# Four PSUM banks for the second layer's first products, and a planner that knows which engine reads a bank

## The chip, the cores and the metric

The program runs on one core of a Trainium2 chip. A core has TensorE (PE, matrix products into the PSUM banks), VectorE (DVE), ScalarE (ACT), GpSimd (POOL) and SyncE (SP, which issues the transfers). The metric is the device time of one execution in microseconds (us). The kernel before took 1287.76 us (median of three runs, 1286.5 to 1288.33).

## The reference, cut to what matters

```python
scores = (q @ k.T) / sqrt(64)              # 4 batches, 8 heads, 768 positions, head size 64
keep   = (key < 4) | ((0 <= query - key) & (query - key < 128))
a      = softmax(where(keep, scores, -1e9))
x      = a @ v                             # as 3072 tokens x 512
h      = maximum(x @ w_in, 0);  y = (h * h) @ w_out         # first layer, 512 -> 2048 -> 512
h      = y @ w2_in;  g = h - tanh(h);  out = g @ w2_out     # second layer, the same sizes
```

Everything is float32. To keep that precision, an operand of a fast product is split into a high and a low part, and one product is made of three matmuls: high x high, high x low, low x high.

## The kernel before

**Tiling.** The first layer runs over 8 blocks of 384 tokens, the second over 6 blocks of 512. In both, the 2048 hidden columns are 16 chunks of 128. For a chunk, `mm_a` (line 567) makes the *first products*: 4 slices of 3 matmuls that add up in one PSUM bank. ACT and DVE turn that bank into g, split in two (`gh` and `gl`, in the second layer `g2h` and `g2l`). Then `mm_b` (line 581) makes the *second products*: 3 matmuls into each of the four banks `acc0` to `acc3`, which add up over all 16 chunks. So a chunk costs TensorE 24 matmuls, of 384 columns in the first layer and of 512 in the second.

**The banks.** There are eight: four `acc`, and `ph`, `S`, `T` and `O`. Attention uses `S` for scores, `T` for transposed weights and `O` for its output; the first layer's first products use `ph`. The second layer's first products use `ph` for even chunks and `S` for odd ones (line 569).

**The second layer's elementwise work** (`step2`, line 627): ACT reads the bank twice (u at L632, th at L633) and makes w from u (L635). DVE makes the mask mk (L639), r from bank and th (L637), w (L641), w times the bank (L643, the last reader of the bank), puts w into r where the mask says so (L645), then g2h (L260) and g2l (L268). The tiles u, th, w and mk have one buffer; r, g2h and g2l have two.

**Attention, as far as it matters here** (`scores` and `values`, lines 311 and 399): TensorE transposes one head's weights into `T` (L358, L359). The readers of `T` are a copy xe (L260 on DVE or L258 on ACT), its remainder (DVE, L370) and three small copies pts. POOL masks xe into pt (L374), and TensorE multiplies pt by the values into `O` (L410 to L415). Instructions of two engines that read the same bank wait for each other, in the order in which the kernel emits them.

**Weights.** A weight arrives as 64-bit words and is turned into two float32 parts by `w_split` (line 534): one instruction on ACT or DVE that reads the transferred words first (L549 or L551), three on DVE (L558, L560, L562), a copy (L258 or L260) and a remainder (L268). The second layer's weights are loaded and split during the last block of the first layer, into the places of the first layer's weights.

**What sets the order.** No order is written by hand. Each operation is put into `Order` with a priority and a cost for each engine that could do it. `solve` (line 124) walks through an imagined time and gives each engine the ready operation with the lowest priority number that it can start soon; where two engines could do an operation, it picks the one that would end sooner. The operations are then emitted in that order, and each engine works through its own list strictly in that order. A change of any cost or priority can therefore move instructions anywhere, and also from one engine to another.

Of the kernel before, what the change touches and what calls it, by code (L numbers as in the profile page):

```python
# [23 lines left out]
B, H, S, D = 4, 8, 768, 64  # L24
P = 128
NT, DM, DFF = B * S, H * D, 2048
NM = DFF // P
NE = DM // P
N1, N2 = 384, 512
NB1, NB2 = NT // N1, NT // N2  # L30
# [8 lines left out]
PLAIN = 2 * H  # L39


REBIAS = 2.0 ** -112


# [16 lines left out]


class Op:
    __slots__ = ("engs", "prio", "emit", "left", "deps", "out", "rank", "ready", "start", "eng", "end")


class C(tuple):
# [10 lines left out]
class Order:  # L78
# [9 lines left out]
    AHEAD = {"V": 1100.0, "D": 400.0}  # L88
    TICK, FIRST = 3413.0, 4590.0
    NEAR = 60.0  # L90
    SAFE = {"T": 250.0}

    def __init__(self):
# [2 lines left out]
    def add(self, engs, prio, reads, writes, emit):  # L96
        op = Op()
        op.engs, op.prio, op.emit, op.deps, op.out, op.rank = engs, prio, emit, set(), [], len(self.ops)
        for k in reads:
            if k in self.writer:  # L100
                op.deps.add(self.writer[k])
            self.readers.setdefault(k, []).append(op)
        for k in writes:
            if k in self.writer:
                op.deps.add(self.writer[k])
            op.deps.update(self.readers.pop(k, ()))
            self.writer[k] = op
        op.deps.discard(op)
        op.deps = sorted(op.deps, key=lambda d: d.rank)
        for d in op.deps:  # L110
            d.out.append(op)
        self.ops.append(op)
# [11 lines left out]
    def solve(self):  # L124
        free = {e: self.AHEAD.get(e, 0.0) for op in self.ops for e in op.engs}
        avail, pend = {e: [] for e in free}, {e: [] for e in free}
        tick = {int(self.FIRST // self.TICK): self.TICK}
        port = 0.0

        def offer(op):  # L130
            for e in op.engs:
                heapq.heappush(pend[e], (op.ready.get(e, 0.0), op.rank, op))

        for op in self.ops:
            op.left, op.ready, op.eng = len(op.deps), {}, None
        for op in self.ops:
            if not op.left:
                offer(op)

        def queue(g, item):  # L140
            return sum(i[2].engs[g][0] / len(i[2].engs) for i in avail[g] if i < item and i[2].eng is None)

        def begin(op, e, now):
            return max(now, port - 60.0) if op.engs[e][2] else now

        done, n = [], len(self.ops)
        while len(done) < n:
            e = min(free, key=lambda g: free[g])
            now, safe = free[e], self.SAFE.get(e, 0.0)
            while pend[e] and pend[e][0][0] <= now:  # L150
                _, r, op = heapq.heappop(pend[e])
                if op.eng is None:
                    heapq.heappush(avail[e], (op.prio, r, op))
            best, held, close, skipped = None, None, None, []
            while avail[e]:
                item = heapq.heappop(avail[e])
                op = item[2]
                if op.eng is not None:
                    continue
                at = begin(op, e, now)  # L160
                if all(max(free[g], op.ready.get(g, 0.0), port if op.engs[g][2] else 0.0) + queue(g, item) + op.engs[g][1] >= at + op.engs[e][1]
                       for g in op.engs if g != e):
                    if at <= now + self.NEAR:
                        if held is None or now + op.engs[e][0] <= held[0] + self.NEAR:
                            if op.ready.get(e, 0.0) + safe <= now:
                                best = item
                                break
                            close = close or item
                    elif held is None and close is None:
                        held = (at, item)  # L170
                skipped.append(item)
            if best is None:
                best = close or (held and held[1])
                if best:
                    skipped.remove(best)
            for item in skipped:
                heapq.heappush(avail[e], item)
            if best is None:
                later = [t for g, t in free.items() if g != e and t > now]
                if pend[e]:  # L180
                    later.append(pend[e][0][0])
                free[e] = min(later) if later else now + 1000.0
                continue
            best = best[2]
            at = begin(best, e, now)
            occ, took = self.clocked(tick, best.engs[e], at) if e == "T" else best.engs[e][:2]
            best.eng, best.start, best.end = e, at, at + took
            free[e] = at + occ
            if best.engs[e][2]:
                port = max(port, at + occ)  # L190
            done.append(best)
            for d in best.out:
                for g in d.engs:
                    d.ready[g] = max(d.ready.get(g, 0.0), best.end + self.hop(e, g))
                d.left -= 1
                if not d.left:
                    offer(d)
        self.order = sorted(done, key=lambda o: o.start)
        return max(op.end for op in done)
# [34 lines left out]
def c_mm(*ns, slow=1):  # L234

    t = sum(slow * (n * 0.4355 + 6.0) for n in ns)
    return C(t, t + 165.0)


class Fast:  # L240
# [144 lines left out]
    def least(self, prio, reads, writes, src, out, nm, half, i, scale):  # L385

        nc = self.nc
        m = self.c["m"][0 if half == 0 and i == 0 else 1 if half == 0 and i == 1 else 2]
        self.o.add({"V": C(222, 375)}, prio, reads, writes,
                   lambda e: nc.vector.tensor_tensor_reduce(out=out(), in0=src(), in1=m, op0=ALU.add, op1=ALU.min, scale=scale,  # L390
                                                            scalar=3.0e38, accum_out=nm()))

# [141 lines left out]
    def w_split(self, layer, m, part, prio, k):  # L534
# [9 lines left out]
        def words(i):  # L544
            return self.wraw[at].rearrange("p (n t) -> p n t", t=2)[:, :, i]

        def rebias(e):
            if e == "A":
                nc.scalar.activation(out=tf, in_=words(1).bitcast(F32), func=AF.Copy, scale=REBIAS)  # L549
            else:  # L550
                nc.vector.tensor_scalar(out=tf, in0=words(1).bitcast(F32), scalar1=REBIAS, scalar2=None, op0=ALU.mult)  # L551

# [13 lines left out]

    def mm_a(self, layer, t, n, prio):
        nc, N = self.nc, (N1, N2)[layer]
        pb = ("ph", 0) if layer == 0 or n % 2 == 0 else ("S", 0)
        x = "x2" if layer else "x"  # L570
        for c in range(NE):
            def emit(e, c=c):
                ph = self.bank[pb]
                w, xh, xl = self.wt[n, 0], self.t[x + "h", t % 2], self.t[x + "l", t % 2]
                for k, (a, b) in enumerate(((0, xh), (0, xl), (512, xh))):
                    nc.tensor.matmul(out=ph[:, :N], lhsT=w[:, a + c * P:a + (c + 1) * P], rhs=b[:, c, :],  # L576
                                     start=(c == 0 and k == 0), stop=(c == NE - 1 and k == 2))
            self.o.add({"T": c_mm(N, N, N)}, prio + 0.1 * c, [("w", n, 0, 0), ("w", n, 0, 1), (x + "h", t % 2, c), (x + "l", t % 2, c)], [pb], emit)
        return pb
# [46 lines left out]

    def step2(self, t, n, v):
        nc, o, T = self.nc, self.o, self.t
        pb = self.mm_a(1, t, n, v)
        k = n % 2  # L630
        th, u, w, mk, r, gh, gl = ("th", 0), ("u", 0), ("w", 0), ("mk", 0), ("r2", k), ("g2h", k), ("g2l", k)
        o.add({"A": c_act(N2, True)}, v + 1.5, [pb], [u], lambda e: nc.scalar.activation(out=T[u], in_=self.bank[pb], func=AF.Square))  # L632
# [238 lines left out]
def general_in(tc, pool, raw, w, out, cst, bank, fl):  # L871
# [25 lines left out]
    for layer in range(2):  # L897
        for m in range(NM):
            for part in range(2):
# [4 lines left out]
                lo, hi, tf = words[:, :, 0], words[:, :, 1], t.bitcast(F32)  # L904
                v.tensor_scalar(out=tf, in0=hi.bitcast(F32), scalar1=REBIAS, scalar2=None, op0=ALU.mult)
                v.tensor_scalar(out=t, in0=t, scalar1=3, scalar2=0x7FFFFFF8, op0=ALU.logical_shift_left, op1=ALU.bitwise_and)
# [157 lines left out]
```

## Time and profile before

| | |
|---|---|
| median of the runs | 1287.76 us (1286.5 to 1288.33) |
| the profiled execution | 1288.81 us, of which the span from first to last instruction is 1286.8 us |
| PE busy | 1255.7 us, 98% of the span |
| DVE, ACT, POOL busy | 1031.0, 630.8 and 152.3 us |
| mean granted clock of TensorE | 0.996 of full speed |

The page of the profile says at the top that TensorE is busy nearly all the time: 1286.8 - 1255.7 = 31.1 us of the span are without a matmul. The share alone doesn't say what those 31.1 us wait for, so the rows further down are taken from the stretches in which they lie. Three views are used. Busy time by stretch gives, for each engine, microseconds and (x) instructions, then the granted clock of TensorE, the share of the transfer engines and GB/s. The timeline gives start, duration, engine, line, operation and tiles; a bracket at its end is the time for which the engine sat idle just before, and the instruction that ended it. The list of waits sums such idle time by pair of lines: microseconds, times, longest.

### The profile page before, as it was taken

How to read it: one execution, taken by the hardware profiler on the slowest of the kernel's cores; microseconds unless marked ns; L12 is line 12 of the kernel's file. 1: busy time of each engine (PE TensorE's matmuls, PEld its weight loads, DVE VectorE, ACT ScalarE, POOL GpSimd, SP SyncE). 2: the span in 40 equal slices, each digit the busy share in tenths (PEclk: the TensorE clock that was granted, in tenths of full speed). 3: DMA queues.
4: the chain of work that ended last, by engine and by line, in shares of the span. 5: the costliest groups of instructions: out<-in, count | busy, mean ns of one | idle time of the engine just before them, and what ended most of it. 6: DMA issues, size and time to landing. Idle time of an engine off the chain costs nothing.

```text
span 1286.8 us, 18762 instructions
## 1 busy us (share of the span) xinstructions
PE 1255.7 (98%) x6568; PEld 1114.6 (87%) x6568; DVE 1031.0 (80%) x2488; ACT 630.8 (49%) x1493; POOL 152.3 (12%) x195
## 2 busy tenths in 40 slices
PE   8899999999999999999999999999999999999997
PEld 5688999999999999999999978888888888888886
DVE  6899997877777777777769999977877877877775
ACT  5655765655555556555535565533433423432332
POOL 1211222222112221122211100000000000000000
PEclk9999999999999999999999999999999999999999
DMA  6884122211222212122118820100100200000000
GB/s 208 276 297 160 32 67 73 84 56 51 75 60 65 76 51 77 52 59 84 28 54 288 286 85 1 36 31 1 66 1 1 66 1 1 34 1 1 33 1 35
DMA packets 41718, 95.01 MB, mean 74 GB/s; under 512 B 4752, under 2 KB 18576, under 8 KB 41616
## 3 DMA queue, kind: packets, MB, share of 16 engines
q1 hardware_dynamic: 41472, 93.34, 22.9%
q8 instruction: 53, 0.87, 0.3%
q10 hardware_dynamic: 144, 0.40, 0.1%
q14 instruction: 49, 0.40, 0.1%
HBM read 79.56 MB, written 14.16 MB: 73 GB/s over the span
## 4 chain that ended last, share of the span: by engine, by line
PE 77%; DVE 10%; issue 5%; DMA 3%; POOL 2%; ACT 2%; DVEq 0%; SPq 0%; ACTq 0%; POOLq 0%
PE ph L576 23%; PE acc L592 21%; PE acc L590 12%; PE S L576 10%; POOL pt L374 2%; PE O L413 2%; PE O L520 2%; DMA yd<-y 1%; DVE wd L560 1%; PE T L358 1%; PE S L324 1%; DMA wr<-w 1%; PE S L325 1%; PE wide L458 1%; PE S L458 1%
## 5 line engine op out<-in xcount | busy, mean ns | idle before, releaser
L576 PE MATMUL ph<-xh,w 128*128 128x384 f32 x1024 | 339.7, 345 | 6.5 <-DVE r L608 3.2
L590 PE MATMUL acc<-gh,w 128*128 128x384 f32 x1024 | 322.4, 339 | 1.5 <-ACT y L258 1.4
L592 PE MATMUL acc<-w,g2h 128*128 128x512 f32 x768 | 299.1, 393 | 1.0 <-DVE g2h L260 1.0
L576 PEld LDWEIGHTS ph<-xh,w 128*128 128x128 f32 x1024 | 192.3, 189 | 10.3 <-DVE r L608 4.7
L590 PEld LDWEIGHTS acc<-gh,w 128*128 128x128 f32 x1024 | 190.5, 188 | 2.4 <-ACT y L258 2.2
L592 PEld LDWEIGHTS acc<-w,g2h 128*128 128x128 f32 x768 | 144.4, 188 | 34.3 <-DVE g2h L260 1.5
L590 PE MATMUL acc<-gl,w 128*128 128x384 f32 x512 | 172.8, 337 | 0.8 <-DVE gl L268 0.7
L576 PE MATMUL ph<-xl,w 128*128 128x384 f32 x512 | 172.3, 337 | 0.4 <-DVE xl L268 0.4
L592 PE MATMUL acc<-w,g2l 128*128 128x512 f32 x384 | 153.0, 398 | 0.7 <-DVE g2l L268 0.7
L576 PE MATMUL ph<-x2h,w 128*128 128x512 f32 x384 | 150.9, 395 | 2.4 <-DVE w L643 2.4
L576 PE MATMUL S<-x2h,w 128*128 128x512 f32 x384 | 151.1, 395 | 0.0
L374 POOL TENSOR_SCALAR_AFFINE_SELECT pt<-xe 128x768 fp32r<-128x768 f32 x96 | 82.6, 885 | 346.5 <-DVE xe L370 346.5
L632 ACT ACTIVATE u<-ph 128x512 f32<-128x512 f32 x48 | 28.7, 598 | 154.5 <-PE ph L576 153.9
L639 DVE TENSOR_SCALAR mk<-u 128x512 uint8<-128x512 f32 x96 | 40.8, 425 | 73.8 <-ACT u L632 73.8
L590 PEld LDWEIGHTS acc<-gl,w 128*128 128x128 f32 x512 | 96.3, 188 | 2.4 <-DVE gl L268 2.2
L576 PEld LDWEIGHTS ph<-xl,w 128*128 128x128 f32 x512 | 97.0, 189 | 1.1 <-DVE xl L268 0.6
L334 ACT ACTIVATE cb<-cb,nm 128x132 f32<-128x132 f32 x144 | 58.3, 405 | 67.0 <-DVE nm L390 65.1
L632 ACT ACTIVATE u<-S 128x512 f32<-128x512 f32 x48 | 28.7, 599 | 125.2 <-PE S L576 124.6
L576 PEld LDWEIGHTS ph<-x2h,w 128*128 128x128 f32 x384 | 72.1, 188 | 19.9 <-DVE w L643 2.7
L592 PEld LDWEIGHTS acc<-w,g2l 128*128 128x128 f32 x384 | 72.2, 188 | 19.4 <-DVE g2l L268 1.3
L576 PEld LDWEIGHTS S<-x2h,w 128*128 128x128 f32 x384 | 72.1, 188 | 17.2
L606 ACT ACTIVATE r<-ph 128x384 f32<-128x384 f32 x115 | 56.4, 491 | 57.0 <-PE ph L576 54.9
(176 smaller groups left out, 2380.6 us busy)
## 6 DMA issues: line engine op xcount, KB each, us to landing
wr<-w SPq DMA_DIRECT2D x64, 512.0 KB, 5.4
raw<-raw SPq DMA_DIRECT2D x32, 454.0 KB, 3.4
raw<-raw SPq DMA_DIRECT2D x31, 390.0 KB, 3.2
yd<-y SPq DMA_DIRECT2D x40, 192.0 KB, 2.0
raw<-yd SPq DMA_DIRECT2D x28, 256.0 KB, 3.2
out<-y SPq DMA_DIRECT2D x20, 256.0 KB, 2.0
raw<-raw SPq DMA_DIRECT2D x24, 160.0 KB, 2.3
raw<-raw SPq DMA_DIRECT2D x24, 128.0 KB, 2.1
```

Of the source, the lines that this page charges most:

```text
L324: nc.tensor.matmul(out=bank[sb][:, :n], lhsT=lhs, rhs=kh[:, col:col + n], start=True, stop=False)
L334: lambda e, i=i: nc.scalar.activation(out=t[cb][:, i, :], in_=t[cb][:, i, :], func=AF.Exp, bias=t[nm][:, i:i + 1], scale=-1.0, accum_out=t ...
L374: lambda e, u=u, s=s, sign=sign, op=op: nc.gpsimd.affine_select(out=t[pt].rearrange("p (n t) q -> p n t q", t=2)[:, 2 * u:, s, :], in_=t[x ...
L413: nc.tensor.matmul(out=oo[:, c:c + cnt * P], lhsT=vv[:, b - 2, :], rhs=pt[:, k + 2 * l:k + 2 * l + 3 * cnt - 2:3, :], start=(n == 0 and l ...
L458: lambda e, i=i, col=N1 + col, n=n: nc.tensor.matmul(out=place(i)[:, :n], lhsT=t["raw", q][:, i * P:(i + 1) * P], rhs=t["raw", q][:, col:c ...
L520: nc.tensor.matmul(out=out[:, c:c + cnt * P], lhsT=v[:, b, :], rhs=t[pp][:, sl:sl + cnt, :], start=(n == 0), stop=False)
L576: nc.tensor.matmul(out=ph[:, :N], lhsT=w[:, a + c * P:a + (c + 1) * P], rhs=b[:, c, :], start=(c == 0 and k == 0), stop=(c == NE - 1 and k ...
L590: nc.tensor.matmul(out=acc[:, :N1], lhsT=w[:, a + e_ * P:a + (e_ + 1) * P], rhs=g, start=st, stop=sp)
L592: nc.tensor.matmul(out=acc, lhsT=g[:, e_ * P:(e_ + 1) * P], rhs=w[:, a:a + 512], start=st, stop=sp)
L606: nc.scalar.activation(out=r, in_=ph, func=AF.Relu)
L632: o.add({"A": c_act(N2, True)}, v + 1.5, [pb], [u], lambda e: nc.scalar.activation(out=T[u], in_=self.bank[pb], func=AF.Square))
L639: lambda e: nc.vector.tensor_scalar(out=T[mk], in0=T[u], scalar1=U_MAX, scalar2=None, op0=ALU.is_lt))
```

## The change

Five edits, all in the planner's model or in what it is told:

1. `mm_a` takes the banks S, O, T and ph in turn for the second layer's chunks, where it took ph and S.
2. The first products of chunks 0 to 2 of the second layer's first block get a priority lower by 25 (earlier), and those of chunks 14 and 15 of its last block one lower by 8.
3. The planner keeps, for each PSUM bank, when and on which engine it was last used, and lets another engine's operation begin only after that (`lock`, `banks`, `begin`).
4. A matmul that follows an idle moment of TensorE is taken to cost 100 ns more (`AFRESH`).
5. The planned time until the result of `least` is there is 296 ns, where it was 375.

The arithmetic is the same, and so is the number of instructions of each kind of work.

```diff
+EARLY = 25.0, 8.0
...
+        op.banks = sorted({k for k in (*reads, *writes) if k[0] in ("acc", "ph", "S", "T", "O", "wide")}) if "T" not in engs else []
...
         def begin(op, e, now):
+            for k in op.banks:
+                end, g = lock.get(k, (0.0, e))
+                if g != e:
+                    now = max(now, end + self.hop(g, e))
             return max(now, port - 60.0) if op.engs[e][2] else now
...
-                if all(max(free[g], op.ready.get(g, 0.0), port if op.engs[g][2] else 0.0) + queue(g, item) + op.engs[g][1] >= at + op.engs[e][1]
+                if all(max(begin(op, g, free[g]), op.ready.get(g, 0.0)) + queue(g, item) + op.engs[g][1] >= at + op.engs[e][1]
...
+            if e == "T" and at > last:
+                occ, took = occ + self.AFRESH, took + self.AFRESH
...
+            for k in best.banks:
+                lock[k] = best.end, e
...
-        self.o.add({"V": C(222, 375)}, prio, reads, writes,
+        self.o.add({"V": C(222, 296)}, prio, reads, writes,
...
-        pb = ("ph", 0) if layer == 0 or n % 2 == 0 else ("S", 0)
+        pb = ("ph" if layer == 0 else ("S", "O", "T", "ph")[n % 4], 0)
...
-        pb = self.mm_a(1, t, n, v)
+        pb = self.mm_a(1, t, n, v - (EARLY[0] if t == 0 and n < 3 else EARLY[1] if t == NB2 - 1 and n >= NM - 2 else 0.0))
```

The order of the instructions differs from the first attention heads on. Three places follow, before and after. Line numbers are 13 higher after the change.

**DVE at the end of the first layer.** `gl` is the low part of the first layer's last chunk. `mk`, the first `r`, `w` and `g2h`, `g2l` belong to chunk 0 of the second layer, `wd` and `w_9`, `w_10`, `w_11` to weights being split, and `y` to the first layer's output. Before, from `gl` on:

```order
L268 TENSOR_TENSOR gl_172<-r_168,gh_170 128x384
L562 SCALAR_TENSOR_TENSOR wd_176<-wr_8_1_7124,wd_176 128x512
L558 TENSOR_SCALAR wd_175<-wd_175 128x512
L260 COPY y_173<-acc_458 128x384
L268 TENSOR_TENSOR w_8_1_7404<-wd_176,w_8_1_7404 128x512
L560 SCALAR_TENSOR_TENSOR wd_175<-wr_10_0_7151,wd_175 128x512
L260 COPY y_174<-acc_459 128x384
L562 SCALAR_TENSOR_TENSOR wd_175<-wr_10_0_7151,wd_175 128x512
L639 TENSOR_SCALAR mk_7369<-u_7367 128x512
L637 TENSOR_TENSOR r_7370<-ph_462,th_7366 128x512
```

and after, from `mk` on:

```order
L652 TENSOR_SCALAR mk_7430<-u_7428 128x512
L575 SCALAR_TENSOR_TENSOR wd_175<-wr_11_0_7246,wd_175 128x512
L650 TENSOR_TENSOR r_7431<-S_476,th_7427 128x512
L281 TENSOR_TENSOR gl_172<-r_168,gh_170 128x384
L654 SCALAR_TENSOR_TENSOR w_7429<-w_7429,u_7428 128x512
L650 TENSOR_TENSOR r_7432<-O_62,th_7427 128x512
L656 TENSOR_TENSOR w_7429<-w_7429,S_476 128x512
L281 TENSOR_TENSOR w_11_0_7467<-wd_175,w_11_0_7467 128x512
L658 COPY_PREDICATED r_7431<-mk_7430,w_7429 128x512
L571 TENSOR_SCALAR wd_176<-wd_176 128x512
L273 CAST g2h_7433<-r_7431 128x512
L652 TENSOR_SCALAR mk_7430<-u_7428 128x512
```

Chunk 0's work began eight rows behind `gl`; now it begins three rows ahead of it, and the weights are further on by then.

**PE at the end of the second layer's last block.** `w_15_0` stands for the first products of the last chunk, `w_12_1` to `w_14_1` for second products. Before, from the last group of first products on:

```order
L576 MATMUL S_463<-x2h_6662,w_15_0_7867 128x512
L576 MATMUL S_463<-x2l_6664,w_15_0_7867 128x512
L576 MATMUL S_463<-x2h_6662,w_15_0_7867 128x512
L592 MATMUL acc_461<-w_13_1_7819,g2h_7373 128x512
L592 MATMUL acc_461<-w_13_1_7819,g2l_7375 128x512
L592 MATMUL acc_461<-w_13_1_7819,g2h_7373 128x512
L592 MATMUL acc_458<-w_14_1_7895,g2h_7372 128x512
```

and after, from the same group on:

```order
L589 MATMUL ph_475<-x2h_6672,w_15_0_7887 128x512
L589 MATMUL ph_475<-x2l_6674,w_15_0_7887 128x512
L589 MATMUL ph_475<-x2h_6672,w_15_0_7887 128x512
L605 MATMUL acc_474<-w_12_1_7764,g2h_7433 128x512
L605 MATMUL acc_474<-w_12_1_7764,g2l_7435 128x512
L605 MATMUL acc_474<-w_12_1_7764,g2h_7433 128x512
L605 MATMUL acc_471<-w_13_1_7850,g2h_7434 128x512
```

The last first products are now made one chunk earlier: ahead of the second products of chunk 15 there stood 15 matmuls (one bank of chunk 13 and all of chunk 14), and now there stand 27.

**DVE at a head's transposed weights in `T`**, in the stretch where attention and first layer run side by side. Before:

```order
L260 CAST gh_170<-r_168 128x384
L260 CAST pts_1249<-T_61 8x128
L268 TENSOR_TENSOR gl_172<-r_168,gh_170 128x384
L370 TENSOR_TENSOR xe_1247<-T_61,xe_1247 128x3x128
L390 ISA cb_1238,nm_1240<-S_463,m_76 128x132
```

and after, at such a head:

```order
L403 ISA nm_1251 128x1
L383 TENSOR_TENSOR xe_1259<-T_61,xe_1259 128x3x128
L273 CAST pts_1262<-T_61 8x128 x2
L273 CAST gh_169<-r_167 128x384
L281 TENSOR_TENSOR gl_172<-r_168,gh_170 128x384
```

Before, every head's remainder of xe came behind all three copies pts. After, it comes ahead of two of them at 14 of the 48 heads. At the other heads it still comes last, mostly with all three copies pts on ACT.

## Rows read from the trace of the kernel before

**Rows 1.** Busy time by stretch, around the layer change, later, and the sum.

```profile
700.00:800.00 100.00, 95.72 (x467) 83.98 (x466) 96.56 (x179) 59.94 (x107) 9.90 (x7) 1.00 0.44 141
800.00:900.00 100.00, 100.00 (x433) 80.89 (x432) 83.88 (x144) 38.83 (x70) 0.00 (x0) 1.00 0.07 22
...
1260.00:1287.00 27.00, 19.67 (x83) 15.03 (x81) 14.02 (x24) 7.43 (x13) 0.00 (x0) 0.94 0.12 42
sum 1287.00, PE 1255.66 PEld 1114.56 DVE 1031.01 ACT 630.78 POOL 152.26; mean PE 59.79 PEld 53.07 DVE 49.10 ACT 30.04 POOL 7.25
```

**Rows 2.** Timeline, TensorE at the start of the second layer.

```profile
742.85 0.34 PE L590 MATMUL acc<-gl,w 128*128 128x384 f32 x1
...
748.74 0.50 PE L576 MATMUL ph<-x2h,w 128*128 128x512 f32 x1 [2.41 <-DVE w L643]
...
752.42 0.50 PE L592 MATMUL acc<-w,g2l 128*128 128x512 f32 x1 [0.43 <-DVE g2l L268]
```

**Rows 3.** Timeline, VectorE at the start of the second layer.

```profile
741.83 0.55 DVE L268 TENSOR_TENSOR gl<-r,gh 128x384 fp32r<-128x384 f32 x1
...
746.14 0.42 DVE L639 TENSOR_SCALAR mk<-u 128x512 uint8<-128x512 f32 x1
746.48 0.68 DVE L637 TENSOR_TENSOR r<-ph,th 128x512 f32<-128x512 f32 x1
...
751.68 0.69 DVE L268 TENSOR_TENSOR g2l<-r,g2h 128x512 fp32r<-128x512 f32 x1
```

**Rows 4.** Chain of waits, start of the second layer (start, duration, engine, tiles).

```profile
743.99 3.89 DMA yd<-y
```

**Rows 5.** Timeline, the end of the second layer.

```profile
1272.87 0.60 ACT L632 ACTIVATE u<-S 128x512 f32<-128x512 f32 x1 [3.88 <-PE S L576]
...
1273.60 0.39 PE L592 MATMUL acc<-w,g2l 128*128 128x512 f32 x1
...
1277.35 0.50 PE L592 MATMUL acc<-w,g2h 128*128 128x512 f32 x1 [1.03 <-DVE g2h L260]
...
1278.08 0.50 PE L592 MATMUL acc<-w,g2l 128*128 128x512 f32 x1 [0.23 <-DVE g2l L268]
```

**Rows 6.** Timeline, one head's transposed weights and what follows.

```profile
316.30 0.30 PE L359 MATMUL T<-idr,ask 128*96 128x128 f32 x1
...
317.21 0.28 DVE L260 CAST pts<-T 8x128 fp32r<-8x128 f32 x1 [0.22 <-ACT xe L258]
...
317.52 0.53 ACT L258 CAST pts<-T 8x128 fp32r<-8x128 f32 x2 [0.35 <-DVE pts L260]
...
318.15 0.56 DVE L370 TENSOR_TENSOR xe<-T,xe 128x384 fp32r<-128x384 f32 x1 [0.66 <-ACT pts L258]
...
320.83 0.50 PE L413 MATMUL O<-pt,vv 128*128 128x256 f32 x2 [0.28 <-POOL pt L374]
```

**Rows 7.** List of waits, TensorE's and VectorE's for such heads.

```profile
PE O L413 <- POOL pt L374: 1.8, 8, 0.3
...
DVE xe L370 <- ACT pts L258: 15.2, 40, 0.7
```

**Rows 8.** Timeline, TensorE's long waits in the first 200 us.

```profile
47.43 0.71 PE L458 MATMUL S<-raw 128*128 128x260 f32 x2 [1.39 <-DVE pnm L390]
...
50.66 0.70 PE L458 MATMUL S<-raw 128*128 128x260 f32 x2 [1.56 <-DVE pnm L390]
...
117.29 0.44 PE L576 MATMUL ph<-xh,w 128*128 128x384 f32 x1 [1.42 <-DVE xh L260]
```

**Rows 9.** Busy time in two stretches of 4 us behind such waits.

```profile
52.00:56.00 4.00, 4.00 (x17) 2.89 (x17) 3.13 (x10) 2.29 (x6) 0.00 (x0) 0.62 0.59 233
120.00:124.00 4.00, 4.00 (x17) 4.00 (x16) 3.47 (x9) 1.57 (x5) 0.00 (x0) 0.59 0.46 122
```

**Rows 10.** Timeline of ScalarE, then the page's table of transfers: weights.

```profile
676.12 0.66 ACT L549 ACTIVATE wd<-wr 128x512 f32<-128x512 f32 x1 [3.40 <-DMA wr<-w]
...
wr<-w SPq DMA_DIRECT2D x64, 512.0 KB, 5.4
```

More of the change, by code (lines that the diff above doesn't have):

```diff
@@ L63 @@
 class Op:
-    __slots__ = ("engs", "prio", "emit", "left", "deps", "out", "rank", "ready", "start", "eng", "end")
+    __slots__ = ("engs", "prio", "emit", "left", "deps", "out", "rank", "banks", "ready", "start", "eng", "end")
 class C(tuple):
@@ L90 @@
     NEAR = 60.0
+    AFRESH = 100.0
     SAFE = {"T": 250.0}
@@ L127, in solve @@
         tick = {int(self.FIRST // self.TICK): self.TICK}
-        port = 0.0
+        port, lock, last = 0.0, {}, 0.0
         def offer(op):
@@ L186, in solve @@
             occ, took = self.clocked(tick, best.engs[e], at) if e == "T" else best.engs[e][:2]
+            if e == "T" and at > last:
+                occ, took = occ + self.AFRESH, took + self.AFRESH
             best.eng, best.start, best.end = e, at, at + took
             free[e] = at + occ
+            if e == "T":
+                last = free[e]
             if best.engs[e][2]:
                 port = max(port, at + occ)
+            for k in best.banks:
+                lock[k] = best.end, e
             done.append(best)
```

## The prediction

> **What bounds the kernel now.** I read busy time by stretch first. The sum row gives TensorE 1255.66 us of work in a span of 1286.8, so 31.1 us are without a matmul, and only there (or where the clock is low) can time be won [rows 1]. From 800 to 900 us, the second layer in its steady course, TensorE is busy for 100.00 of 100 us at a granted clock of 1.00, with 433 matmuls, 0.231 us each; the reader should see that nothing waits there, though two banks serve the first products. From 700 to 800 us, at the layer change, it is different: DVE is busy for 96.56 us and TensorE for 95.72, so DVE, which splits weights, ends the first layer and begins the second, sets the pace.
>
> The timelines then name the waits. At the start of the second layer, first products stand 2.41 us until DVE's last reader of `ph` (L643) is done, and second products 0.43 us for g2l: 2.84 us [rows 2]. At the end, chunk 15's second products wait 1.03 us for g2h and 0.23 us for g2l: 1.26 us [rows 5]. The list of waits has 8 waits of the value products for POOL's pt, 1.8 us together [rows 7]. Ahead of 200 us there are three long ones, 1.39, 1.56 and 1.42 us, all on DVE [rows 8], and behind them two stretches of 4 us at a granted clock of 0.62 and 0.59 [rows 9]: a mix of the two levels, 2.4 and 1.2 GHz, following TensorE's idle moments, which costs 4 x 0.38 = 1.5 and 4 x 0.41 = 1.6 us.
>
> **The change, part by part.**
>
> *Steady second layer: 0.* Four banks instead of two give each chunk's readers more time, but TensorE has no idle time to give back there [rows 1]. The Trainium skill ("Perfetto Trace Analysis", section "Optimizing Tensor Performance", "Matmuls") says that independent matmul groups should rotate through different PSUM banks, so that emptying one overlaps the next group; by that sentence the whole layer would gain, and the 100.00 busy us show that two banks already give that overlap here.
>
> *The end.* Chunk 15's bank is read from 1272.87 on, and its g2h releases TensorE at 1277.35: 4.48 us [rows 5]. Before, 15 matmuls stand between its last first product and its second products, 15 x 0.231 = 3.5 us; after, 27, so 12 x 0.231 = 2.8 us more cover against 1.26 us of wait. The first matmul behind each wait also lasts 0.50 instead of 0.39 us [rows 5], 0.2 us for two. Chunks 13, 14 and 15 now come closer together on DVE, whose tiles u, th, w and mk have one buffer; the first products of 13 and 14 finish 0.7 us apart, by the matmuls that stand between them in the order. Adding the durations of the DVE steps in that order leaves some 0.7 to 1 us of the cover over. I take -1.5. Bounds: -1.5, or +0.5 if chunk 15's elementwise work is pushed back by more than the cover.
>
> *The start of the second layer.* Lost now: 2.84 plus 0.2 for two first matmuls of 0.50 us, 3.0. After, chunks 0, 1 and 2 make their first products during the first layer's last chunks, in S, O and T, and chunk 3 in `ph`, so no bank has to be emptied before the second products of the last first-layer chunk. Is DVE on time for these, with three chunks' elementwise work now mixed in? In the order TensorE has 30 more matmuls ahead of them (30 x 0.231 = 6.9 us later) and DVE has 14 more instructions ahead of `gl`; at 96.56 / 179 = 0.54 us each [rows 1] 7.5, by their kinds 7.1. `gl` now ends at 742.38 [rows 3] and is used at 742.85 [rows 2], 0.47 us of lead; 0.1 to 0.6 us of shift use up some or all of that. Next come chunk 0's second products: g2l begins 9 rows behind `gl`, 9 x 0.54 = 4.9 us, where it now begins at 751.68, 9.85 us behind [rows 3]. TensorE has 12 matmuls of 384 columns (0.175 us apart, 2.1) and 9 of 512 (2.1) to do in between, 4.2 us. So it may wait up to 0.3 to 0.6 us there. The output copies y, which empty the four `acc` banks, stand in the way too: their transfer takes 3.89 us [rows 4], and y has two buffers, so the third and fourth copies, DVE's among them, may be late by 0 to 1 us. I leave 1.1 us lost: gain 1.9. Bounds: -3.1 (nothing lost), +0.5 (a copy y that waits on DVE's list and holds `gl`'s successors too).
>
> *Attention's `T` bank.* In the head shown, from the transposing matmul at 316.30 to the value products at 320.83 it takes 4.53 us, through a chain that hops between ACT and DVE since both read `T` [rows 6]; VectorE sits 15.2 us in 40 such waits [rows 7], which matters only where TensorE waits at the end, 1.8 us in 8. In the new order, where less TensorE work than about 4.5 us lies between, the remainder of xe precedes two of the copies pts (0.6 to 1 us off the chain); the others have more. I take -1.3 of the 1.8. Bounds: -1.8, +0.7 (half a wait per head at the same eight places, 0.1 us each: the largest now is 0.3).
>
> *The first 200 us.* At the places of the three waits of [rows 8] the order of TensorE's rows is the same and DVE's steps ahead of them alike, so 0; but attention's front is replanned, and a wait there shifts by its own size: 1.4 to 1.6 either way, with a clock dip of 1.5 that comes or goes: -3 to +3.
>
> *The rest: 0.* About 40 instructions move from DVE to ACT; ACT is busy for 630.78 us of the span [rows 1].
>
> Sum: -1.5 - 1.9 - 1.3 = -4.7. The profiled execution took 1288.81 us, the median of the runs is 1.05 lower: 1287.76 - 4.7 = 1283.1.
>
> **The rivals.**
>
> *R1, the same DVE work waits elsewhere: 1286.3.* DVE is busy for 96.56 of 100 us at the layer change [rows 1]. If what TensorE no longer waits for on a bank it waits for on gl and g2l, since DVE's list has no slack, the start gains nothing; the value products likewise wait for POOL behind another reader. Only the end's 1.5 is left. For it speaks the DVE share, against it that DVE still stands idle for 3.44 of these 100 us, which steps issued earlier can fill.
>
> *R2, slower, weights: 1291.* In the order DVE now does 6 of the first weight steps that touch transferred words, before 2 (the rest on ACT). A transfer takes 5.4 us to land, and ACT stood 3.40 us for one [rows 10]. When DVE stands, `gl`, r and g2l stand behind it in its list, and TensorE behind them. Two such waits are 6.8 us; this decides once they exceed the 4.7 of the forecast: 1283.1 + 6.8 + about 1 for a clock dip = 1291. Against it: DVE was idle for only 3.44 of these 100 us, so most words are there in time.
>
> *R3, more gained: 1280.1.* If the wait at 117 us (1.42) [rows 8] and the clock dip behind it (1.6) [rows 9] dissolve with the new order, 3.0 more goes. The same local order speaks against it.
>
> *R4, the clock: 1292.* If the rotation let TensorE's clock drop at the start of each of six second-layer blocks, 6 x 1.5 = 9 us [rows 9]. Against it: at 800 to 900 us the target bank already changes every 3 matmuls, first to second products and back, at a clock of 1.00 and with no idle time [rows 1]. The Trainium skill ("TensorE: Matmul & The Clock Gate", section "A second HAM failure mode: psum-queue depth-cycling") describes a kernel whose cycling through banks made TensorE idle in short moments and its clock oscillate; that would be this rival.
>
> **How the numbers follow.** Forecast 0.53, R3 0.10, R1 0.22, R2 0.11, R4 0.04. A difference of 0.2%, 2.6 us, is about what a measurement of this kernel can tell from none. Faster by more: the forecast and R3, 0.63. Within: R1, 0.22. Slower: R2 and R4, 0.15. The likeliest's own range is 1280.3 to 1285.2, from its bounds taken together; the range for 8 times in 10 goes from R3 with one more wait of 1.5 gone to between R1 and R2: 1278.6 to 1289.2.
>
> **What would show it.** The end: no gap on TensorE between the last first product and the end. The start: a gap of up to about 1 us, with g2l or a copy y named, in place of 2.41 for L643 (then L656). Attention: fewer than 8 waits for pt, under 0.5 us together. Steady second layer: still 100.00, the clock 1.00. If the sum is right and these are not, I was lucky; a new wait of over 2 us between 700 and 760 us, or DVE waiting for transferred weights there, makes the forecast wrong, and so would waits before 200 us of other sizes than [rows 8].

## The result, and the profile after

The changed kernel took 1266.95 us (median of four runs, 1265.11 to 1269.36), the kernel before beside it 1288.05: ratio 0.9839, 95% interval 0.982 to 0.9858. The forecast was 1283.1 with a range down to 1278.6, so the direction was right and the size wrong: 21.1 us came off where 4.7 were forecast. The profiled spans are 1286.8 and 1263.1 us, 23.7 apart.

Busy time by stretch of the changed kernel (us, TensorE busy and its matmuls, then weight loads, DVE, ACT, POOL, granted clock, share of the transfers, GB/s) answers [rows 1]:

```profile
700.00:800.00 100.00, 99.92 (x470) 85.16 (x470) 99.72 (x187) 59.61 (x106) 0.00 (x0) 1.00 0.30 95
800.00:900.00 100.00, 100.00 (x432) 80.87 (x432) 81.52 (x138) 37.52 (x67) 0.00 (x0) 1.00 0.11 32
...
1240.00:1263.10 23.10, 17.51 (x76) 13.81 (x74) 12.21 (x21) 7.67 (x13) 0.00 (x0) 0.94 0.14 49
sum 1263.10, PE 1244.08 PEld 1113.16 DVE 1023.16 ACT 644.24 POOL 143.22; mean PE 59.24 PEld 53.01 DVE 48.72 ACT 30.68 POOL 6.82
```

The sum row holds the surprise. The span lost 23.7 us, but TensorE's idle time only 31.1 - 19.0 = 12.1; the other 11.6 went out of its *busy* time, though the same 6568 matmuls are made at the same clock. So "busy" held waits. One view of one stretch tells where. From 200 to 700 us, where attention and the first layer run side by side, before:

```profile
200.00:700.00 500.00, 494.40 (x3007) 481.54 (x3007) 377.74 (x1149) 276.40 (x748) 100.50 (x124) 1.00 0.25 75
```

and after:

```profile
200.00:700.00 500.00, 498.75 (x3071) 494.06 (x3070) 388.71 (x1133) 296.21 (x804) 101.25 (x125) 1.00 0.28 83
```

TensorE's busy time rose by 4.4 us, but 64 more matmuls fitted in, and the weight loads' busy time rose by 12.5 us. How a wait hides is seen in one head of the kernel before (timeline, TensorE and its weight loads):

```profile
287.81 0.33 PE L590 MATMUL acc<-gl,w 128*128 128x384 f32 x1
...
287.99 0.34 PE L590 MATMUL acc<-gh,w 128*128 128x384 f32 x1
288.48 0.30 PEld L413 LDWEIGHTS O<-pt,vv 128*128 128x128 f32 x2 [0.47 <-POOL pt L374]
288.48 0.50 PE L413 MATMUL O<-pt,vv 128*128 128x256 f32 x2
288.70 0.19 PEld L410 LDWEIGHTS O<-pt,vv 128*128 128x128 f32 x1
288.82 0.28 PE L410 MATMUL O<-pt,vv 128*128 128x256 f32 x1
```

A matmul of 384 columns is shown as busy for 0.34 us, but the next one starts 0.17 to 0.18 us after it. Here the next one starts 0.49 us later, 0.32 late, and the matmul's own row shows no bracket, since the row before seems to cover most of it. The weight load's row does show it: 0.47 us for POOL's pt.

So I went from start to start instead: each matmul's distance to the next one, less that of an undisturbed matmul of its width (0.173 us for 384 columns, 0.230 for 512, 0.117 for 256, 0.118 for 260). The undisturbed course adds up to 1197 us in both kernels; what lies beyond it is 82.4 us before and 58.9 after, 23.5 less, nearly the whole difference of the spans. The levels hang on what is taken for the narrower matmuls (with other choices 200 to 700 us holds from 16.6 to 38.3 us before); the differences do not, that stretch loses 12.8 us with each of them. By stretch (us beyond the undisturbed course; "locks and banks" is an experiment further down):

| stretch | before | after | difference | forecast | locks and banks |
|---|---|---|---|---|---|
| 0 to 200, front | 47.5 | 43.3 | -4.2 | 0 | 40.4 |
| 200 to 700, attention with first layer | 22.2 | 9.4 | -12.8 | -1.3 | 9.2 |
| 700 to 760, layer change | 5.9 | 1.6 | -4.3 | -1.9 | 0.4 |
| 760 to 1240, second layer | 4.6 | 4.4 | -0.2 | 0 | 4.3 |
| 1240 to the end | 2.2 | 0.2 | -2.0 | -1.5 | 0.2 |

The profiled execution of before (1288.81 us) lies above its median and that of the changed kernel (1265.11) is the fastest of its four, so the differences of this table come out some us larger than those of the medians.

From 200 to 700 us, delays ahead of the value products (O) fell from 7.3 to 0.4 us, ahead of second products (acc) from 5.1 to 1.5, ahead of scores (S) from 3.5 to 1.2. The weight loads' list of waits (us in total, times, longest) says the first of these directly. Before:

```profile
PEld O L413 <- POOL pt L374: 8.7, 19, 0.6
```

and after:

```profile
PEld O L426 <- POOL pt L387: 0.6, 4, 0.2
```

The list of the matmuls' own waits had 1.8 us in 8 for the same thing [rows 7]. What became of a head, in the changed kernel's timeline, answers [rows 6]:

```profile
318.28 0.30 PE L372 MATMUL T<-idr,ask 128*96 128x128 f32 x1
318.67 0.48 ACT L271 CAST xe<-T 128x384 fp32r<-128x384 f32 x1 [0.17 <-PE T L372]
319.05 0.79 ACT L271 CAST pts<-T 8x128 fp32r<-8x128 f32 x3
319.93 0.56 DVE L383 TENSOR_TENSOR xe<-T,xe 128x384 fp32r<-128x384 f32 x1 [0.34 <-issue]
320.56 1.78 POOL L387 TENSOR_SCALAR_AFFINE_SELECT pt<-xe 128x768 fp32r<-128x768 f32 x2 [8.48 <-DVE xe L383]
...
322.90 0.39 PE L426 MATMUL O<-pt,vv 128*128 128x256 f32 x2
```

All three copies pts follow xe on ACT, in 0.79 us; before, the readers of T went ACT to DVE to ACT to DVE. From the first reader's start to the end of xe's remainder the median head took 2.02 us before and takes 1.76 after. DVE's longest wait of [rows 7], 15.2 us in 40, is halved:

```profile
DVE xe L383 <- ACT pts L271: 7.5, 26, 1.2
```

The value products start 4.62 us after the transposes, with 4.5 us of other matmuls between. Before, 18 of 48 heads had only 3.7 or 4.0 us of matmuls there and 21 had 4.3; after, 35 have 4.5 us or more (before 9), and the 11 with 3.7 or 4.0 all have the remainder of xe ahead of two copies pts.

The end has no wait left on TensorE: the timeline from 1238 us on shows no bracket on its rows, where [rows 5] had 1.26 us. By the lists of waits, DVE waits for no transferred weights, and ACT once, 3.0 us at 659 us, before the layer change.

### The profile page after: what moved, and what is told of

It reads as the page before. It is cut to its first block, busy times and chain, and to the rows that moved or that the text cites. A ratio compares the mean times of both kernels' runs of the same rounds, so it can differ in the third digit from the quotient of the medians.

```text
span 1263.1 us, 18806 instructions
## 1 busy us (share of the span) xinstructions
PE 1244.1 (98%) x6568; PEld 1113.2 (88%) x6568; DVE 1023.2 (81%) x2453; ACT 644.2 (51%) x1541; POOL 143.2 (11%) x192
## 4 chain that ended last, share of the span: by engine, by line
PE 88%; DVE 7%; issue 2%; ACT 1%; DMA 1%; POOL 0%; DVEq 0%; POOLq 0%; ACTq 0%
PE ph L589 23%; PE acc L605 21%; PE acc L603 18%; PE T L589 5%; PE S L589 5%; PE O L589 5%; PE O L426 2%; PE S L338 1%; PE S L337 1%; PE T L371 1%; PE O L533 1%; DVE wd L573 1%; DVE wd L575 1%; DVE w L281 1%; PE O L428 1%
## 5 line engine op out<-in xcount | busy, mean ns | idle before, releaser
L605 PE MATMUL acc<-w,g2h 128*128 128x512 f32 x768 | 295.8, 396 | 0.0
L619 ACT ACTIVATE r<-ph 128x384 f32<-128x384 f32 x120 | 59.1, 492 | 80.4 <-PE ph L589 78.8
L589 PE MATMUL T<-x2h,w 128*128 128x512 f32 x192 | 75.0, 390 | 0.0
L589 PE MATMUL O<-x2h,w 128*128 128x512 f32 x192 | 74.9, 391 | 0.0
L589 PE MATMUL S<-x2h,w 128*128 128x512 f32 x192 | 74.7, 391 | 0.0
L589 PE MATMUL ph<-x2h,w 128*128 128x512 f32 x192 | 74.6, 391 | 0.0
L658 DVE COPY_PREDICATED r<-mk,w 128x512 f32<-128x512 uint8 x96 | 71.9, 749 | 2.7
L281 DVE TENSOR_TENSOR gl<-r,gh 128x384 fp32r<-128x384 f32 x128 | 70.9, 554 | 2.5 <-ACT gh L271 1.5
```

What stands on the lines that cost most here:

```text
L281: (nc.vector if e == "V" else nc.gpsimd).tensor_tensor(out=out, in0=a, in1=b.bitcast(F32), op=ALU.subtract)
L605: nc.tensor.matmul(out=acc, lhsT=g[:, e_ * P:(e_ + 1) * P], rhs=w[:, a:a + 512], start=st, stop=sp)
L619: nc.scalar.activation(out=r, in_=ph, func=AF.Relu)
L658: lambda e: nc.vector.copy_predicated(out=T[r], mask=T[mk], data=T[w]))
```

## The experiments

Times are medians beside the kernel before on the same chip: 1285.64 us for the first four, 1286.37 for the next four, 1286.01 for the last three. "Beyond the undisturbed course" always stands against the profile of before shown above. Where a diff below has the changed kernel's lines taken back, it is against the changed kernel.

**Locks only.**

```diff
-    AFRESH = 100.0
+    AFRESH = 0.0
-EARLY = 25.0, 8.0
+EARLY = 0.0, 0.0
-        self.o.add({"V": C(222, 296)}, prio, reads, writes,
+        self.o.add({"V": C(222, 375)}, prio, reads, writes,
-        pb = ("ph" if layer == 0 else ("S", "O", "T", "ph")[n % 4], 0)
+        pb = ("ph", 0) if layer == 0 or n % 2 == 0 else ("S", 0)
```

> The kernel before with edit 3 alone: the planner knows that two engines can't read one PSUM bank at a time; the old banks, no priorities, no AFRESH, the old time for least. From start to start of TensorE's matmuls, 200 to 700 us holds 22.2 us beyond the even course before and 9.4 after the change. Theory L (the locks removed that): 200 to 700 us falls to about 9 to 11, the front by 2 to 4, start and end of the second layer stay as before: 1270 to 1275 us. Rival F (the matmul behind an idle moment priced higher did it): 1285 to 1289. Rival S (the gain needs all edits together, it is the luck of one order): anywhere over 1278.

Measured: 1270.29 us, 15.4 below, ratio 0.9881 (0.9862 to 0.99). Beyond the undisturbed course 200 to 700 us holds 10.9 us (before 22.2), the layer change 5.4 and the end 2.0 (before 5.9 and 2.2): theory L. The front gained 9.6, far more than the 2 to 4 expected; the profiled execution is the fastest of the four here too. The same stretch of its profile as above:

```profile
200.00:700.00 500.00, 497.41 (x3065) 494.39 (x3065) 377.11 (x1089) 313.55 (x856) 102.22 (x125) 1.00 0.27 85
```

3065 matmuls and 494.39 us of weight loads: edit 3 alone has the changed kernel's middle, and F and S fall. In its order 37 of 48 heads read T as ACT, ACT, ACT, ACT, DVE; before, one did.

**Banks and priorities only.**

```diff
-        op.banks = sorted({k for k in (*reads, *writes) if k[0] in ("acc", "ph", "S", "T", "O", "wide")}) if "T" not in engs else []
+        op.banks = sorted({k for k in (*reads, *writes) if k[0] in ()})
-    AFRESH = 100.0
+    AFRESH = 0.0
-        self.o.add({"V": C(222, 296)}, prio, reads, writes,
+        self.o.add({"V": C(222, 375)}, prio, reads, writes,
```

> The kernel before with edits 1 and 2 alone: four banks and the early priorities, no change to the planner's model. The order up to about 650 us is that of before. Theory L: only the start of the second layer (5.9 to 1.6 us beyond the even course) and its end (2.2 to 0.2) get better, 5 to 6.3 us: 1281.5 to 1283. Rival: without the locks the start of the second layer gets a new wait on DVE, and only the end's 2 us are left: about 1286.

Measured: 1280.21 us, 5.4 below, ratio 0.9955 (0.9939 to 0.997). The layer change holds 2.5 us (before 5.9), the end 0.3 (2.2), the stretches up to 700 us are those of before (22.9 us from 200 to 700), so the comparison of two engines in `solve`, which stays in its new form here, changes nothing there. What I had forecast as start plus end, 3.4 us, measures 5.3. Its list of the weight loads' waits has the waits of [rows 7] in full:

```profile
PEld O L426 <- POOL pt L387: 8.7, 19, 0.6
```

**The change without the locks.** The first pair of lines of the diff above, alone, in the changed kernel.

> The changed kernel with edit 3 alone undone. Theory L: the value products wait for POOL again, 200 to 700 us goes back from 9.4 to about 18 to 22 us beyond the even course, start and end stay good: 1276 to 1281. Rival F: AFRESH and the new time for least keep most of the gain: 1267 to 1270.

Measured: 1278.96 us, 6.7 below before, ratio 0.9948 (0.9932 to 0.9964). From 200 to 700 us 18.9 us, layer change and end 2.0 and 0.2. The middle's waits are back, most of them:

```profile
PEld O L426 <- POOL pt L387: 6.4, 17, 0.6
```

**Value products one group later.** The kernel before and its own order, in which only these products are moved:

```diff
+    def late(order):
+        for op in [o for o in order if o.tag == "pv"]:
+            i = order.index(op)
+            j = i + 1
+            while op not in order[j].deps and order[j].eng != "T":
+                j += 1
+            if op not in order[j].deps and order[j].tag in ("emit_a", "emit_b"):
+                order.insert(j, order.pop(i))
...
             self.est = self.o.solve()
+            self.late(self.o.order)
```

> The kernel before in its own order, but a head's value products stand behind the next group of three first or second products where one follows them at once (21 of 48 heads, among them the 16 with 3.98 us of other matmuls since the transposed weights); nothing else moves. If the wait for POOL's pt is a real loss of 0.2 to 0.45 us per head at those 16, as the starts of the matmuls say, this gains 4 to 6 us: 1282 to 1284. If the list of TensorE's waits is right, which puts it at 1.8 us in 8 waits, it gains 1 to 2: 1286 to 1287. If the wait only moves on to the next group: 1288.

Measured: 1281.4 us, 4.2 below, ratio 0.9961 (0.9946 to 0.9976). The time is within 4 to 6; the trace bears this out only in part. The weight loads' list has two of the 19 waits left:

```profile
PEld O L414 <- POOL pt L375: 1.1, 2, 0.5
```

Beyond the undisturbed course, the delays ahead of O from 200 to 700 us fell by 6.3 us, but the stretch by only 2.9, since delays moved on, mostly to first products (2.5 us; 600 to 700 us as a whole rose by 1.1). Net of that it is still more than the 1.8 us of the matmuls' own list. The front fell by 4.2, and that was not traced to a wait.

**The change without edits 4 and 5: locks and banks.**

```diff
-    AFRESH = 100.0
+    AFRESH = 0.0
-        self.o.add({"V": C(222, 296)}, prio, reads, writes,
+        self.o.add({"V": C(222, 375)}, prio, reads, writes,
```

> The changed kernel with edits 4 and 5 undone: locks, four banks and early priorities stay. The locks alone took 15.4 us off, banks and priorities alone 5.4 (each against the same runs of before). Theory A (the two act at different places, so they add up, and edits 4 and 5 are worth nothing): 20 to 22 us below before, and ahead of 200 us no wait of 1.4 to 1.6 us on pnm, as with the locks alone. Rival: edits 4 and 5 are needed to keep the start of the second layer short: 16 to 18 us below before.

Measured: 1260.0 us, 26.4 below, ratio 0.9799 (0.9786 to 0.9812): more than either theory had. By the profiles the parts nearly add up (locks 21.5 and banks with priorities 4.8 less beyond the undisturbed course, both together 27.9); the medians, 15.4 and 5.4, fall short of 26.4, and I can't say why the run with the locks alone has its median 3 us above its lowest run. As theory A expected, the two long waits on pnm ahead of 200 us are gone:

```profile
40.00:60.00 20.00, 19.63 (x113) 16.09 (x112) 18.65 (x56) 14.27 (x39) 5.13 (x7) 1.00 0.93 337
```

113 matmuls where the kernel before made 82 and the changed one 91. The layer change holds 0.4 us.

**No priorities.**

```diff
-EARLY = 25.0, 8.0
+EARLY = 0.0, 0.0
```

> The changed kernel with edit 2 alone undone: four banks, but no early priorities. If the priorities make both gains at the layer's start and end, the end's 1.3 us of waits comes back and the start loses 2 to 4 us: 15 to 18 us below before. If the banks alone make the start's gain: 19 to 20 us below before, with only the end's wait back.

Measured: 1270.51 us, 15.9 below before, ratio 0.988 (0.9865 to 0.9895). The time fits the first theory, the trace the second: the layer change is as short without the priorities (1.5 us, changed kernel 1.6), so the banks make that gain; the end's waits are back as they were:

```profile
1258.85 0.50 PE L605 MATMUL acc<-w,g2h 128*128 128x512 f32 x1 [1.02 <-DVE g2h L273]
1259.58 0.50 PE L605 MATMUL acc<-w,g2l 128*128 128x512 f32 x1 [0.23 <-DVE g2l L281]
```

Another 2.4 us appeared from 600 to 700 us, ahead of first products; that was not followed up.

**Copies pts on ACT only**, in the kernel before, with its model as it was.

```diff
-            self.copy(d - 6, [tb], [("pts", k2, i)], lambda i=i: (t["pts", k2][0:8, i * P:(i + 1) * P], bank[tb][32 * i:32 * i + 8, 3 * P:]), P, True)
+            o.add({"A": c_copy(P, True)["A"]}, d - 6, [tb], [("pts", k2, i)],
+                  lambda e, i=i: nc.scalar.copy(out=t["pts", k2][0:8, i * P:(i + 1) * P], in_=bank[tb][32 * i:32 * i + 8, 3 * P:]))
```

> The kernel before, but the three small copies pts may only go to ACT; the planner's model is unchanged and doesn't know of locks. It replans: the readers of T alternate less, and about 4.7 us of other matmuls lie between the transposed weights and the value products at most heads, before 4.0 to 4.3. Theory: waits of the value products fall from 7.3 to under 1 us by the starts of the matmuls, 5 to 8 us below before. Rival (it is the locks' knowledge of S and ph that counts, not T): 0 to 2 us below before.

Measured: 1272.7 us, 13.7 below, ratio 0.9893 (0.9878 to 0.9908), beyond what the theory expected. 200 to 700 us holds 12.2 us (before 22.2), the front 42.1 (47.5), layer change and end are as before. No wait for pt is left in the list of the weight loads' waits. One line that keeps the three copies pts on ACT does most of what the planner's locks do. It replans the order, though, so it changes more than this chain.

**The old time for least** (edit 5 alone undone: the second pair of lines of the diff under locks and banks).

> The changed kernel with edit 5 alone undone (least at 375 ns), so locks, banks, priorities and AFRESH. If edit 5 is worth nothing: 20 to 22 us below before. If the new time for least is what brought the waits on pnm ahead of 200 us back (2.6 us, which the locks alone had not): 23 to 25 us below before.

Measured: 1263.4 us, 23.0 below, ratio 0.9825 (0.9812 to 0.9839). It differs from locks and banks by AFRESH alone and is 3.4 us slower than that on the same chip, so edit 4 costs time here; the front holds 41.7 us against 40.4, the layer change 1.7 against 0.4. The gain is at the lower end of the second theory's 23 to 25, and the trace bears that theory out: the waits of scores for pnm are 0.3 us in all, 2.6 in the changed kernel.

**The changed kernel, locks and banks, and the copies too, on one chip.** The last is locks and banks with the copies pts on ACT only.

> The changed kernel itself once more, beside the next two on one chip. 20 to 22 us below before, as at first.

> The changed kernel without edits 4 and 5 once more. If these two edits really cost time in the first 200 us, it stays 3 to 6 us below the changed kernel on the same chip; if the difference was the chip's, 0 to 2.

> As before this one (locks, four banks, priorities), and the three copies pts may only go to ACT. If the locks gained by keeping the readers of T on one engine, most of that is had already, where 37 of 48 heads read T in the order ACT, ACT, ACT, ACT, DVE: within 2 us of the kernel without this. If copies on DVE still cost something at the other 11 heads: 2 to 4 us less.

Measured: the changed kernel 1268.48 us (0.9866, 0.9851 to 0.9881), 17.5 below before and so short of the 20 to 22 expected, locks and banks 1259.87 (0.9799, 0.9786 to 0.9813), with the copies 1261.69 (0.9808, 0.9795 to 0.9822). The changed kernel without edits 4 and 5 beats both kernels: 8.6 us below the changed one, more than the 3 to 6 expected, and 26.1 below before. By the starts it is 6.3 us, 4.8 of them in the front and 1.2 at the layer change. Forcing the copies adds nothing to the locks, as it should if both act on the same readers of T.

## Why the prediction was wrong

**Attention's T bank: "I take -1.3 of the 1.8".** This is the term that failed. The mechanism was named rightly (readers of one bank hop between engines, the remainder comes late, the value products wait for pt), but it was sized from the list of the matmuls' waits, 1.8 us in 8, with -1.8 as its bound. The starts of the matmuls say 7.3 us, the weight loads' list 8.7 us in 19; 7.3 fell to 0.4. The same reading missed the delays ahead of second products and scores, 8.6 us together, of which 5.9 went: this term's stretch gave 12.8 us. Locks only and the change without the locks show that edit 3 does it.

That the hops on T are the root of most of it rests on comparing runs. Value products one group later and the change without the locks leave the chain of T's readers as long as before (median 2.01 us) and gain 2.9 and 3.3 us from 200 to 700 us. Locks only, copies on ACT only and the changed kernel have it at 1.76 us and gain 11.3, 10.0 and 12.8. VectorE's idle time ahead of its own readers of T in this stretch goes the same way: 27.6 us before, 27.1 and 23.1 in the first two runs, 15.1, 13.1 and 15.3 in the other three. All of these but value products one group later also replan everything else, so how much is the chain itself, how much VectorE being free sooner for what second products and scores need, and what the locks do at S and ph beside it, no run took apart.

**"TensorE 1255.66 us of work in a span of 1286.8, so 31.1 us are without a matmul, and only there (or where the clock is low) can time be won".** This step put the bound on everything behind it and was wrong: 11.6 of the 23.7 us came out of the busy time. All the prediction's bounds at their best add up to -9.4 us, 1278.4, so no choice within them reaches the measured time. The 1.00 clock and 98.9 busy us from 200 to 300 us looked full, like 800 to 900; the latter was full (433 matmuls at 0.231 us apart), the former was not.

**The start of the second layer: "I leave 1.1 us lost: gain 1.9".** Right in mechanism, too small: 4.3 us less from 700 to 760, of which banks and priorities alone give 3.4 and the locks' order the rest. By the starts, the two waits that the prediction lists cost 3.4 us and went altogether, where 1.1 was to be left; another 2.1 us, ahead of first-layer first products at 702 and 720 us, are not in its sum and went as well. TensorE had no wait on a copy y or on transferred weights; what is left is 0.7 us at gl of earlier chunks and 0.25 at g2l. DVE was as full as R1 said (99.72 of 100 us busy), and TensorE lost no more than this to it.

**The end: -1.5.** Right: 2.0 by the starts, and no priorities brings the 1.25 us of waits back. The 0.2 for two first matmuls behind a wait is what they cost (0.11 each). What the sum left out is 0.16 us of each wait that the row before covers.

**The front: "0", with -3 to +3.** It gave 4.2, outside these bounds; locks and banks, without edits 4 and 5, gave 7.1 there. The dip of the clock at 52 us is gone, and the one behind the wait at 117 us is longer, from 116 us on behind a wait of 1.5 us for ACT (stretches of the changed kernel, answering [rows 9]):

```profile
52.00:56.00 4.00, 4.00 (x25) 3.68 (x24) 3.90 (x16) 1.49 (x6) 0.00 (x0) 1.00 0.51 148
116.00:124.00 8.00, 7.48 (x24) 6.50 (x25) 7.84 (x19) 3.03 (x8) 0.00 (x0) 0.57 0.48 135
```

**The rivals.** R2 and R4 did not happen: no DVE wait for weights, and the clock is 1.00 from 700 to 1240 us with four banks. R3 happened in part, at 40 to 60 us instead of 117. None of them had a gain of over 8 us, since all were capped by the 31.1 us and by the same list of waits. The signs named for the end, the start, attention and the steady layer came true, but they are signs of brackets and say nothing of size.

## What to carry to other kernels

Where matmuls are pipelined, TensorE's busy share hides waits shorter than a matmul's shown latency: count matmuls per stretch, look at the idle time of the weight loads, or take the distance from start to start before calling a stretch full. A planner that lets two engines read one bank at once plans a chain shorter than the one that runs; here that was so at most heads, and each place cost too little to see by itself. And a change made of several edits is worth taking apart: here two of the five cost 8.6 us.

## What the runs showed of the hardware

A wait on TensorE cost more than itself here: the two matmuls that start at 288.48 and 288.70 us took 0.34 us to the next start (288.82), where two undisturbed ones take 0.23, so 0.32 us of wait became 0.42. The extra is the same at every such place: at all 35 delays of 0.19 to 2.58 us from 200 to 1240 us in the kernel before, for matmuls of the four widths above, the first one behind the delay took 0.103 to 0.109 us longer to the next start. Many short waits thus cost more than one long wait of the same sum. Readers of one bank on two engines went one after the other here, with 0.2 to 0.7 us of idle time ahead of each on its engine [rows 6]; three copies in a row on ACT took 0.79 us. Four banks in turn left TensorE's clock at 1.00 in every stretch of the second layer's steady course.
